# A gated recurrence and a mixer on one core: the last batch's transposes by DMA, and a batch's inputs loaded ahead of the second weight

## The chip, the core and the metric

The kernel runs on one core of a Trainium2 chip. A core has five engines that run their own instruction queues side by side: TensorE (PE, matrix products into PSUM), VectorE (DVE), ScalarE (ACT), GpSimd (POOL) and SyncE (SP, which here only starts transfers). Sixteen DMA engines carry the transfers. The on-chip memory is SBUF with 128 partitions, and PSUM with 8 banks, where PE writes its results. A semaphore makes one engine wait for another. The metric is the time of one execution in microseconds (us); less is better.

## The reference

Four batches (B), eight heads (H), 768 time steps (S), head dimension 48 (D). The first part is a recurrence with a gate alpha, the second a mixer: a low-rank mix over time, then a two-layer network over the 384 channels.

```python
    for t in range(S):
        state = alpha[:, :, t, :, None] * state + np.einsum('bhd,bhe->bhde', k[:, :, t], v[:, :, t])
        y[:, :, t] = np.einsum('bhd,bhde->bhe', q[:, :, t], state)
...
    x = np.ascontiguousarray(attn_out.transpose(0, 2, 1, 3)).reshape(B, S, H * D)
...
    xt = x.transpose(0, 2, 1)
    h = xt @ U @ V
    u = x + h.transpose(0, 2, 1)
    ch = np.maximum(u @ w_ch1, 0.0) @ w_ch2
    return (u + ch).astype(np.float32)
```

x is 4 x 768 x 384, U and V have rank 32 and act over time, the two layers go from 384 to 1536 channels and back. All inputs and the output are float32.

## The kernel before

**Tiling.** Time is cut in six chunks of 128 steps, taken two at a time, so a batch has three groups. Within a chunk the recurrence is written with matrix products. The logarithm of alpha is summed over time by a product with a triangle of ones (L358; L360 gives the chunk's total). Exponentials of plus and minus that sum (`aa`, `ai`) scale q and k (`rq`, `rk`, L374). Both are transposed so that the head dimension lies on the partitions (`qT`, `kT`): PE transposes eight 128x128 blocks into a PSUM bank (L383), and ACT or DVE copies the bank to SBUF (L289, L291). Then come the scores (L406), a mask on DVE (`pm`, L416), the state (L441, L448, L451) and y (L468, L474), which ACT copies into `xb` (L486). `rv` is v cast to bf16 on POOL (L291).

After a batch's three groups comes the mix, `stage_mix`: a product with U over all six chunks (L499), its copy `utx`, then for each chunk a product with V (L524) that DVE adds to `xb` (L525). That gives u. PE transposes u in three blocks of six (L534), ACT copies them to `uT` (L542). The two layers are `mlp1` (L553, 72 matmuls a batch of 384 columns, in two halves of time of 36, with a ReLU on ACT or DVE, L563 and L565) and `mlp2` (L574, again 72), whose result DVE adds to u in one of three `ou` buffers (L583) and SP stores (L584). The first batch does u's transposes in another way (L515, L518).

**Loads.** Each batch has four loads of 1.2 MB in the order alpha, k, q, v, each into one of six `io` buffers (L327). Between the first and the second batch's come U, V (four copies) and the weights in three parts each, w1 and w2, through two parts to an `io` buffer; POOL casts them to bf16.

**What sets the order.** Each step is an operation handed to a planner with its engine, a cost in ns and a priority (`P.add`). The planner simulates all engines with these costs, always takes the step that can start first (and the lowest priority number among those), gives it its buffers, and so writes each engine's fixed order. On the chip each engine follows its own order and waits by semaphores. SP in particular takes its transfers strictly in turn: one that waits for its data holds all behind it. For SP the planner keeps a clock of the sequencer and one of the transfers:

```python
            if eng == "SP":
                clock[eng] = max(t + 450.0, dma)
                dma = max(dma, t + 1200.0) + op.cost
                op.end = dma + 1700.0
```

Loads have the batch's number as priority (alpha of batch b: b, k: b + 0.1, and so on), the parts of w1 0.5, of w2 0.6, the stores -1. Attention steps have 1000 to 1110, the mix 500 to 530, the layers 5000 and up, so PE fills with the layers of one batch the time in which the next batch's recurrence waits.

Of the kernel before, what the change touches and what calls it, by code (L numbers as in the profile page):

```python
# [49 lines left out]
class Op:  # L50
    __slots__ = ("eng", "cost", "fn", "prio", "deps", "bufs", "n", "end", "users", "est", "i")


class Plan:
# [11 lines left out]
    def add(self, eng, cost, fn, r=(), w=(), prio=0.0, after=(), kind=None):  # L66
        op = Op()
        op.eng, op.cost, op.fn, op.prio = eng, cost, fn, prio
        op.i = len(self.ops)
# [31 lines left out]
    def run(self):  # L101
# [13 lines left out]
        while todo:  # L115
# [73 lines left out]
def kernel(  # L189
# [12 lines left out]
    nc = tc.nc  # L202
# [37 lines left out]
    u_in = const.tile([128, NC, R], FP32, name="u_in")  # L240
    vm_in = const.tile([128, S], FP32, name="vm_in")
# [16 lines left out]
    pms = Pool(slots("pm", 4, [C, 2, HP, C], BF16))  # L258
# [3 lines left out]
    uts = Pool(slots("uT", 2, [128, NCT, S], BF16))  # L262
# [17 lines left out]
    mlps = [every, every, every, every]  # L280
# [12 lines left out]
    def load_low_rank():  # L293
        P.add("SP", 500, lambda: nc.sync.dma_start(u_in, moe_U.rearrange("(c p) r -> p c r", p=128)), w=["u_in"], prio=0.3)
        for g in range(4):
            P.add("SP", 400, lambda g=g: nc.sync.dma_start(vm_in[32 * g : 32 * g + R, :], moe_V), w=[("vm_in", g)], prio=0.3)
        P.add("POOL", 350, lambda: nc.gpsimd.tensor_copy(u_sb, u_in), r=["u_in"], w=["u"], prio=300)
        P.add("POOL", 820, lambda: nc.gpsimd.tensor_copy(vm_sb, vm_in), r=[("vm_in", g) for g in range(4)], w=["vm"], prio=300)

    def load_big():  # L300
# [6 lines left out]
        for i, (src, dst) in enumerate(parts):  # L307
# [7 lines left out]
            P.add("SP", 2000, lambda src=src, stage=stage: nc.sync.dma_start(stage(), src), w=[(t, i)], prio=0.5 if i < 3 else 0.6)  # L315
# [14 lines left out]
    def stage_gla(b, g, sprev, xb, ins):  # L330
# [8 lines left out]
        eq = "DVE" if first else "POOL"  # L339
        ev = "POOL"  # L340
        eqt = "ACT" if first else "DVE"
        split = (-1, 1, 1)[g] if first else -1
# [47 lines left out]
        for src, dst, eng, cost in ((rk, kT, "ACT", 1015), (rq, qT, eqt, 1015 if eqt == "ACT" else 640)):  # L390
            tb = Buf(gen)
# [100 lines left out]
    def stage_mix(b, xb, uT):  # L492
# [14 lines left out]
        if b == 0:  # L507
            P.fill_end = op
            for hf in range(2):
                for j in range(NCT):  # L510
# [9 lines left out]
                    P.add(eng, 550 if eng == "DVE" else 490, lambda hf=hf, j=j, tb=tb, eng=eng: copy(eng, uT()[:, j, hf * TW : (hf + 1) * TW], tb()[:, 0, 0:TW]), r=[tb], w=[(uT, hf, j)], prio=pr)  # L520
# [112 lines left out]
```

## Time and profile before

| | us |
|---|---|
| median of 3 runs | 181.5 (180.69 to 182.88) |
| the profiled execution | 180.38 |
| its span, first to last instruction | 178.7 |
| PE busy in the span | 166.2 |
| POOL, DVE, ACT busy | 52.7, 94.0, 86.5 |

The profiled execution lies a little under the fastest of the three runs. Its span is 1.7 us shorter than its time. The mean granted clock of TensorE is 0.989 of full speed.

How to read it: the page cuts the span into 40 slices of 4.5 us and gives each engine's busy share in tenths. A window row gives the same for a stretch that is named in us. A row of the time order gives start and length of an instruction, the idle time of its engine before it and, after the arrow, what ended that idle time. The chain follows, from the last instruction back, what each waited for. Of the loads, the first rows that use a tile tell when it had landed.

### The profile page before, as it was taken

Reading aid. Unit: us, or ns where it says so; the run is one execution under the profiler, and the core shown is the slowest. Engines: PE = TensorE matmul, PEld = TensorE weight load, DVE = VectorE, ACT = ScalarE, POOL = GpSimd, SP = SyncE. Lnnn points to the kernel's source line nnn. Section 1 sums busy time; section 2 is a strip of 40 time slices with the busy share of each in tenths; the row PEclk is TensorE's granted clock in tenths of the full one; section 3 lists DMA queues with packets and bytes.
Section 4 is the critical chain, followed back from the end, with each engine's and each line's share of the span. In section 5 each row is a group of like instructions: output and inputs, shape, how many; then the busy total and the mean of one; then the engine's idle time right before and its main releaser. Section 6 shows DMA issues by size and latency. Waiting matters only on the chain.

```text
span 178.7 us, 4275 instructions
## 1 busy us (share of the span) xinstructions
PE 166.2 (93%) x1821; PEld 107.8 (60%) x1821; DVE 94.0 (53%) x159; ACT 86.5 (48%) x142; POOL 52.7 (29%) x52
## 2 busy tenths in 40 slices
PE   5997888999999996988999999999999999999992
PEld 4775665555666754655666566755566565656560
DVE  2022991643327775458676577667485432544421
ACT  2387684645891344894783847401555310422200
POOL 4000197760469600497416567000000000000000
PEclk9999999999999999699999999999999999999999
DMA  4987999996977868899889300111101112101212
GB/s 111 262 257 221 261 287 391 370 321 191 261 224 225 254 204 246 275 259 262 257 230 252 117 15 33 48 46 44 48 0 44 48 46 88 44 0 48 85 49 88
DMA packets 32068, 29.08 MB, mean 163 GB/s; under 512 B 1584, under 2 KB 30768, under 8 KB 32048
## 3 DMA queue, kind: packets, MB, share of 16 engines
q1 hardware_dynamic: 32048, 28.81, 53.5%
q8 instruction: 14, 0.23, 0.6%
q14 instruction: 6, 0.05, 0.1%
HBM read 24.08 MB, written 4.72 MB: 161 GB/s over the span
## 4 chain that ended last, share of the span: by engine, by line
PE 65%; DMA 17%; SPq 6%; DVE 5%; ACT 3%; issue 2%; POOL 1%; DVEq 0%; ACTq 0%; POOLq 0%
PE ps L553 24%; PE ps L574 22%; DMA io<-in_alpha_dram 7%; DMA io<-in_q_dram 6%; SPq L327 4%; DMA io<-in_v_dram 4%; PE ps L474 3%; PE ps L383 3%; DVE pm L416 3%; PE ps L406 3%; SPq L584 2%; PE ps L468 2%; PE ps L441 1%; PE ps L524 1%; ACT lt L350 1%
## 5 line engine op out<-in xcount | busy, mean ns | idle before, releaser
L553 PE MATMUL ps<-uT,w_sb 128*128 128x384 bf16 x288 | 52.9, 326 | 0.0
L574 PE MATMUL ps<-w_sb,h1t 128*128 128x384 bf16 x288 | 52.4, 326 | 0.0
L563 ACT ACTIVATE h1t<-ps 128x384 bf16<-128x384 f32 x48 | 23.7, 493 | 37.7 <-PE ps L553 37.4
L574 PEld LDWEIGHTS <-h1t 128*128 128x128 bf16 x288 | 27.2, 98 | 17.1 <-issue 0.3
L553 PEld LDWEIGHTS <-w_sb 128*128 128x128 bf16 x288 | 26.9, 98 | 16.2 <-issue 0.3
L565 DVE TENSOR_SCALAR h1t<-ps 128x384 bf16<-128x384 f32 x48 | 26.7, 557 | 16.6 <-PE ps L553 14.8
L416 DVE TENSOR_TENSOR pm<-ps,maskc 128x1024 bf16<-128x1024 f32 x22 | 26.8, 1221 | 5.5 <-PE ps L406 4.9
L583 DVE TENSOR_TENSOR ou<-xb,ps 128x384 f32<-128x384 bf16 x24 | 13.3, 553 | 29.2 <-PE ps L574 20.5
L374 POOL TENSOR_TENSOR rk<-io,ai 128x768 bf16<-128x768 f32 x9 | 14.8, 1643 | 25.7 <-ACT ai L368 18.9
L289 ACT COPY kt<-ps 128x1024 bf16<-128x1024 bf16 x12 | 12.1, 1015 | 13.1 <-PE ps L383 6.1
L291 POOL CAST rv<-io 128x768 bf16<-128x768 f32 x12 | 9.6, 829 | 23.6 <-DMA io<-in_v_dram 23.6
L486 ACT CAST xb<-ps 128x768 bf16<-128x768 f32 x12 | 9.6, 798 | 13.8 <-PE ps L474 13.7
L374 POOL TENSOR_TENSOR rq<-io,aa 128x768 bf16<-128x768 f32 x9 | 14.8, 1645 | 4.1 <-DMA io<-in_q_dram 2.1
L587 PE MATMUL ps<-fill_in,ident 128*128 128x256 bf16 x87 | 13.6, 316 | 1.9 <-POOL ident masks.py:199 1.9
L350 ACT ACTIVATE lt<-io 128x768 bf16<-128x768 f32 x12 | 9.6, 841 | 9.7 <-DMA io<-in_alpha_dram 9.7
L525 DVE TENSOR_TENSOR xb<-xb,ps 128x384 bf16<-128x384 bf16 x18 | 9.5, 550 | 6.0 <-PE ps L524 5.9
L587 PEld LDWEIGHTS <-ident 128*128 128x128 bf16 x87 | 9.4, 113 | 4.1 <-POOL ident masks.py:199 1.9
L368 ACT ACTIVATE ai<-ps 128x768 bf16<-128x768 f32 x12 | 9.9, 822 | 0.3 <-PE ps L360 0.3
L369 ACT ACTIVATE aa<-ps 128x768 bf16<-128x768 f32 x12 | 10.0, 830 | 0.0
L291 POOL CAST w_sb<-io 128x1536 bf16<-128x1536 f32 x6 | 8.8, 1469 | 3.9 <-DMA io<-in_moe_w_ch_dram 3.9
L474 PE MATMUL ps<-rv,pm 128*128 128x48 bf16 x192 | 8.9, 184 | 1.1 <-DVE pm L416 1.1
L406 PE MATMUL ps<-qt,kt 48*128 48x128 bf16 x192 | 9.0, 218 | 0.5 <-ACT xb L486 0.5
(57 smaller groups left out, 157.4 us busy)
## 6 DMA issues: line engine op xcount, KB each, us to landing
io<-in_moe_w_ch_dram SPq DMA_DIRECT2D x6, 768.0 KB, 9.7
out_dram<-ou SPq DMA_DIRECT2D x24, 192.0 KB, 1.9
vm_in<-in_moe_V_dram SPq DMA_DIRECT2D x4, 96.0 KB, 2.6
u_in<-in_moe_U_dram SPq DMA_DIRECT2D x1, 96.0 KB, 6.1
io<-in_alpha_dram SPq DMA_DIRECT2D x4, 0.2 KB, 11.3
io<-in_k_dram SPq DMA_DIRECT2D x4, 0.2 KB, 10.2
io<-in_q_dram SPq DMA_DIRECT2D x4, 0.2 KB, 10.5
io<-in_v_dram SPq DMA_DIRECT2D x4, 0.2 KB, 8.9
```

The source lines that it names most:

```text
L289: nc.scalar.copy(dst, src)
L291: ENG[eng].tensor_copy(dst, src)
L374: ENG[eng].tensor_tensor(dst()[:, :, :, 0:D], ch(src), fac().rearrange("t g (h d) -> t g h d", d=D), op=ALU.mult)
L406: nc.tensor.matmul(s2[:, par, p, :], lhsT=kT()[o : o + D, i, p, :], rhs=qT()[o : o + D, i, p, :], start=(p == 0), stop=(p == HP - 1),)
L416: nc.vector.tensor_tensor(pmi().rearrange("t two hp c -> t (two hp) c"), sc().rearrange("p two (hp c) -> p (two hp) c", c=C), maskc.to_bro ...
L474: nc.tensor.matmul(y2[:, par, p, :], lhsT=pm[i]()[:, par, p, :], rhs=rv()[:, i, 2 * p + par, :], start=(i == 0 and p == 0 and last is None ...
L553: nc.tensor.matmul(hb()[:, 0, 0:TW], lhsT=w1_sb[:, ct, jt * 128 : (jt + 1) * 128], rhs=uT()[:, ct, tt * TW : (tt + 1) * TW], start=(ct == ...
L563: P.add("ACT", 500, lambda jt=jt, hb=hb: nc.scalar.activation(h1()[:, jt, :], hb()[:, 0, 0:TW], AF.Relu), r=[hb], w=[(h1, jt)], prio=100)
L565: P.add("DVE", 560, lambda jt=jt, hb=hb: nc.vector.tensor_scalar_max(h1()[:, jt, :], hb()[:, 0, 0:TW], 0.0), r=[hb], w=[(h1, jt)], prio=100)
L574: nc.tensor.matmul(hb()[:, 0, 0:DM], lhsT=h1()[:, jt, (c % 3) * C : (c % 3 + 1) * C], rhs=w2_sb[:, jt, :], start=(jt == 0), stop=(jt == NJ ...
L583: P.add("DVE", 550, lambda: nc.vector.tensor_tensor(ou(), xb()[:, c, :], hb()[:, 0, 0:DM], op=ALU.add), r=[hb, (xb, c)], w=[ou], prio=100)
L587: P.fill_fn = lambda i: nc.tensor.matmul(ps[:, i, 0:256], lhsT=ident, rhs=fill_in, start=True, stop=True)
```

## The change

Four things are changed in what runs, and the planner's order follows from them.

1. In the last batch (b = 3), k's and q's transposes of all three groups are done by SP as DMA transposes from `rk` and `rq` into `kT` and `qT`, in place of PE's eight blocks and a copy each. u's transposes in that batch are two DMA transposes of three chunks each, in place of three PE blocks and copies. `uT` is laid out chunk by chunk for that.
2. In the second batch (b = 1), q is scaled on DVE and no longer on POOL, and q's transposed blocks are copied by ACT and no longer by DVE.
3. The parts of w2 get priority 1.15 in place of 0.6, so that alpha and k of the second batch (1.0 and 1.1) go ahead of them.
4. U and V go through an `io` buffer and not tiles of their own; there are six `pm` buffers in place of four. The matmul that adds the mix at the end of `mlp2` in the first batch is a step of its own. Priorities of the first batch's `mlp1` are closer together, so all of it can stand ahead of `mlp2`.

The planner is told for a DMA transpose how long it holds SP (`hold`).

```diff
-                clock[eng] = max(t + 450.0, dma)
+                clock[eng] = max(t + op.hold, dma)
...
-    pms = Pool(slots("pm", 4, [C, 2, HP, C], BF16))
+    pms = Pool(slots("pm", 6, [C, 2, HP, C], BF16))
...
-    uts = Pool(slots("uT", 2, [128, NCT, S], BF16))
+    uts = Pool(slots("uT", 2, [128, NC, NCT, C], BF16))
...
-        P.add("SP", 500, lambda: nc.sync.dma_start(u_in, moe_U.rearrange("(c p) r -> p c r", p=128)), w=["u_in"], prio=0.3)
+        P.add("SP", 500, lambda: nc.sync.dma_start(u_in(), moe_U.rearrange("(c p) r -> p c r", p=128)), w=[(t, 4)], prio=0.3)
...
-            P.add("SP", 2000, lambda src=src, stage=stage: nc.sync.dma_start(stage(), src), w=[(t, i)], prio=0.5 if i < 3 else 0.6)
+            P.add("SP", 2000, lambda src=src, stage=stage: nc.sync.dma_start(stage(), src), w=[(t, i)], prio=0.5 if i < 3 else 1.15)
...
-        eq = "DVE" if first else "POOL"
+        eq = "DVE" if b in (0, 1) else "POOL"
         ev = "POOL"
-        eqt = "ACT" if first else "DVE"
+        eqt = "ACT" if b in (0, 1) else "DVE"
...
         for src, dst, eng, cost in ((rk, kT, "ACT", 1015), (rq, qT, eqt, 1015 if eqt == "ACT" else 640)):
+            if b in (3,):
+                P.add("SP", 1000, lambda src=src, dst=dst: nc.sync.dma_start_transpose(dst().rearrange("p g e c -> p (g e) c"), src().rearrange("t g h w -> t (g h w)")), r=[src], w=[dst], prio=pr / 1000 - 1, hold=1250.0)
+                continue
...
+            if b in (3,):
+                if c % 3 == 2:
+                    P.add("SP", 1100, lambda c=c: nc.sync.dma_start_transpose(uT()[:, c - 2 : c + 1].rearrange("p c j t -> p (c j) t"), xb()[:, c - 2 : c + 1, :].rearrange("p c m -> p (c m)")), r=[(xb, c - i) for i in range(3)], w=[(uT, c // 3, j) for j in range(NCT)], prio=pr / 1000 - 1, hold=1300.0)
+                continue
...
-            pr = 5000 + b * 1000 + tt * 100 + jt * 8
+            pr = 5000 + b * 1000 + tt * (100 if b else 50) + jt * (8 if b else 4)
...
-                        rhs=uT()[:, ct, tt * TW : (tt + 1) * TW], start=(ct == 0), stop=(ct == NCT - 1),
+                        rhs=uT()[:, 3 * tt : 3 * tt + 3, ct, :], start=(ct == 0), stop=(ct == NCT - 1),
```

How the order moves: first SP's queue from V's copies on, at the end of the first batch's loads. A row is the line, the transfer with the tile written and the one read, and their shape; `w_ch` are the weights, 3x512 a part of w1, 4x384 of w2; `io` buffers are told apart by their number. Before:

```order
L296 DMA vm_in<-in_moe_V_dram 32x768 x4
L315 DMA io_90<-in_moe_w_ch_dram 128x3x512 x2
L315 DMA io_91<-in_moe_w_ch_dram 128x3x512
L315 DMA io_91<-in_moe_w_ch_dram 128x4x384
L315 DMA io_86<-in_moe_w_ch_dram 128x4x384 x2
L327 DMA io_87<-in_alpha_dram 128x48x48
L327 DMA io_88<-in_k_dram 128x48x48
L327 DMA io_89<-in_q_dram 128x48x48
L584 DMA out_dram<-ou_149 128x384
L584 DMA out_dram<-ou_150 128x384
L327 DMA io_90<-in_v_dram 128x48x48
L327 DMA io_91<-in_alpha_dram 128x48x48
```

The same place in the changed kernel:

```order
L321 DMA io_89<-in_moe_w_ch_dram 128x3x512 x2
L321 DMA io_84<-in_moe_w_ch_dram 128x3x512
L333 DMA io_85<-in_alpha_dram 128x48x48
L333 DMA io_86<-in_k_dram 128x48x48
L321 DMA io_84<-in_moe_w_ch_dram 128x4x384
L321 DMA io_87<-in_moe_w_ch_dram 128x4x384 x2
L333 DMA io_88<-in_q_dram 128x48x48
L333 DMA io_89<-in_v_dram 128x48x48
L333 DMA io_84<-in_alpha_dram 128x48x48
L596 DMA out_dram<-ou_149 128x384
```

Alpha and k have moved ahead of w2's three parts, and v and the third batch's alpha ahead of the stores, of which three now follow together.

Second, POOL's queue from the cast of w1 on, through the second batch. Before:

```order
L291 CAST w_sb<-io_91 128x3x512
L291 CAST w_sb<-io_91 128x1536
L291 CAST w_sb<-io_86 128x1536 x2
L374 TENSOR_TENSOR rk_101<-io_88,ai_118 128x16x48
L374 TENSOR_TENSOR rk_98<-io_88,ai_119 128x16x48
L374 TENSOR_TENSOR rq_95<-io_89,aa_115 128x16x48
L374 TENSOR_TENSOR rq_96<-io_89,aa_116 128x16x48
L374 TENSOR_TENSOR rk_99<-io_88,ai_120 128x16x48
L374 TENSOR_TENSOR rq_97<-io_89,aa_117 128x16x48
L291 CAST rv_112<-io_90 128x768
```

In the changed kernel:

```order
L289 CAST w_sb<-io_84 128x3x512
L380 TENSOR_TENSOR rk_99<-io_86,ai_116 128x16x48
L289 CAST w_sb<-io_84 128x1536
L380 TENSOR_TENSOR rk_96<-io_86,ai_117 128x16x48
L289 CAST w_sb<-io_87 128x1536 x2
L380 TENSOR_TENSOR rk_97<-io_86,ai_118 128x16x48
L289 CAST rv_110<-io_89 128x768
```

The casts of w2 (128x1536) now stand between the three k products of the second batch, and the three q products have left POOL. In the third batch POOL now does the third k product ahead of its first cast of v, and in the last one all casts of v ahead of the third group's k and q.

Third, SP's queue from the last batch's v on, where there were only stores before:

```order
L333 DMA io_85<-in_v_dram 128x48x48
L398 DMA_TRANSPOSE kt_123<-rk_97 128x8x128
L596 DMA out_dram<-ou_149 128x384
L398 DMA_TRANSPOSE qt_126<-rq_93 128x8x128
L398 DMA_TRANSPOSE kt_124<-rk_98 128x8x128
L596 DMA out_dram<-ou_150 128x384
L398 DMA_TRANSPOSE qt_127<-rq_94 128x8x128
L398 DMA_TRANSPOSE kt_125<-rk_99 128x8x128
L398 DMA_TRANSPOSE qt_128<-rq_95 128x8x128
L596 DMA out_dram<-ou_151 128x384
```

The six transposes of k and q stand behind the last load, with stores of the second batch between them. u's two follow later among the third batch's stores.

On PE, the 66 transposes of the last batch are gone (48 for k and q, 18 for u), and the rest is dealt out anew. All 72 matmuls of the first batch's `mlp1` now stand ahead of the first of its `mlp2`. Between the mixes (L499) of the second and the third batch PE's queue held 51 matmuls of `mlp1` and 12 of `mlp2`; now it holds 60 and 24, one block of sums (L358) more and two blocks of eight transposes less. The last batch's first scores stand after the third batch's mix, three matmuls of `mlp1` and eight of `mlp2` between them.

More of the change, by code (lines that the diff above doesn't have):

```diff
@@ L50 @@
 class Op:
-    __slots__ = ("eng", "cost", "fn", "prio", "deps", "bufs", "n", "end", "users", "est", "i")
+    __slots__ = ("eng", "cost", "fn", "prio", "deps", "bufs", "n", "end", "users", "est", "i", "hold")
 class Plan:
@@ L279 @@
     mlp0 = banks((6,), (7,), (4,), (5,))
-    mlps = [every, every, every, every]
+    mlps = [banks(*[(i,) for i in s]) for s in (range(8),) * 4]
     def bf(bank):
@@ L569, in mlp2 @@
         pr = 5000 + b * 1000 + 100 + (c % 3) * 33 + (0 if c < 3 else 100)
-        for g in range(3):
+        for g in range(NJ // 4):
             def f(g=g):
-                for jt in range(4 * g, 4 * g + 4):
+                for jt in range(4 * g, 4 * (g + 1)):
                     nc.tensor.matmul(
@@ L577, in f @@
                     )
-                if g == 2 and utx is not None:
-                    nc.tensor.matmul(hb()[:, 0, 0:DM], lhsT=vm_sb[:, c * C : (c + 1) * C], rhs=utx(), start=False, stop=True)
-            P.add("PE", mm(*[DM] * (5 if g == 2 and utx is not None else 4)), f, r=([utx] if utx is not None else []) + [(h1, jt) for jt in range(4 * g, 4 * g + 4)] + [("w2", g)], w=[hb], prio=pr + g)
+            P.add("PE", mm(*[DM] * 4), f, r=[(h1, jt) for jt in range(4 * g, 4 * (g + 1))] + [("w2", g * 4 // 4)], w=[hb], prio=pr + g)
+        if utx is not None:
+            P.add("PE", mm(DM), lambda: nc.tensor.matmul(hb()[:, 0, 0:DM], lhsT=vm_sb[:, c * C : (c + 1) * C], rhs=utx(), start=False, stop=True), r=[utx], w=[hb], prio=pr + 9)
         ou = Buf(outs)
```

34 lines of the change are left out of this document (18 added, 16 removed).

## The prediction

> **What bounds the kernel now.** I read the page's busy shares and slices first, then the chain that ended last, then the windows in which PE (TensorE) is not full, and last the time order of the engines in those windows. The page:
>
> ```profile
> PE 166.2 (93%) x1821; PEld 107.8 (60%) x1821; DVE 94.0 (53%) x159; ACT 86.5 (48%) x142; POOL 52.7 (29%) x52
> PE   5997888999999996988999999999999999999992
> PEclk9999999999999999699999999999999999999999
> PE 65%; DMA 17%; SPq 6%; DVE 5%; ACT 3%; issue 2%; POOL 1%; DVEq 0%; ACTq 0%; POOLq 0%
> ```
>
> PE is busy for 93% of the 178.7 us; no other engine is above 60%. The chain is PE for 65% and transfers and their queue (DMA, SPq) for 23%. Where each rules is in the windows (columns: length; busy us and count of PE, weight loads, DVE, ACT, POOL; granted clock, DMA share, GB/s):
>
> ```profile
> 65.00:70.00 5.00, 3.71 (x85) 2.60 (x84) 3.85 (x6) 2.99 (x4) 0.00 (x0) 1.00 0.86 246
> 72.00:77.00 5.00, 4.46 (x39) 3.03 (x36) 2.86 (x6) 4.11 (x8) 3.06 (x2) 0.66 0.80 236
> 80.00:85.00 5.00, 3.97 (x64) 2.54 (x57) 4.26 (x6) 2.35 (x5) 3.87 (x5) 1.00 0.91 257
> 85.00:90.00 5.00, 5.00 (x86) 3.09 (x83) 3.44 (x7) 4.01 (x7) 1.97 (x2) 1.00 0.85 243
> 110.00:120.00 10.00, 10.00 (x114) 6.45 (x112) 5.72 (x11) 2.96 (x6) 0.98 (x1) 1.00 0.09 32
> ```
>
> From 85 us on PE has no idle time: matmuls taken out there shorten the kernel by their own length. Between 65 and 85 us PE idles 1.29 us in the first row, 0.54 in the second and 1.03 in the third, and in the second its clock is 0.66, which costs another 0.34 x 5 = 1.7 us. Up to the load of the third part of w1, at about 28 us, the order of no queue changes. What PE waits for between 65 and 85 us stands in the time order of POOL (start, length, instruction, idle time before it and its releaser):
>
> ```profile
> 34.40 1.47 POOL L291 CAST w_sb<-io 128x1536 bf16<-128x1536 f32 x1 [0.66 <-DMA io<-in_moe_w_ch_dram]
> 46.98 3.42 POOL L374 TENSOR_TENSOR rk<-io,ai 128x768 bf16<-128x768 f32 x2 [6.71 <-PE ps L553]
> 51.97 3.25 POOL L374 TENSOR_TENSOR rq<-io,aa 128x768 bf16<-128x768 f32 x2 [1.56 <-DMA io<-in_q_dram]
> 59.03 2.37 POOL L291 CAST rv<-io 128x768 bf16<-128x768 f32 x3 [0.62 <-DMA io<-in_v_dram]
> 81.41 1.60 POOL L291 CAST rv<-io 128x768 bf16<-128x768 f32 x2 [1.13 <-DMA io<-in_v_dram]
> 95.55 1.64 POOL L374 TENSOR_TENSOR rq<-io,aa 128x768 bf16<-128x768 f32 x1 [0.58 <-DMA io<-in_q_dram]
> 100.08 2.37 POOL L291 CAST rv<-io 128x768 bf16<-128x768 f32 x3 [2.89 <-DMA io<-in_v_dram]
> ```
>
> POOL waits for loads: v of the second batch lands at 59.03 us, of the third at 81.41, q and v of the last at 95.55 and 100.08. So the loads set the pace up to 85 us, and PE after it.
>
> **Term 1: transposes off PE, -3.7 us.** The last batch loses six blocks of 8 transposes (k and q of three groups) and three blocks of 6 (u), 66 matmuls. In the chain (start, length, what) they cost, among neighbours that PE runs without a gap:
>
> ```profile
> 97.87 0.45 PE ps L383 x8
> 111.64 0.34 PE ps L534 x6
> 128.24 0.43 PE ps L499 x6
> 169.27 5.86 PE ps L574 x36
> ```
>
> 6 x 0.45 + 3 x 0.34 = 3.7 us. In the program before, the last batch's stand in the full stretch: the chain's last piece on PE, from 169.27, ends without a wait. All 3.7 us are on the path, unless a transfer that replaces them comes late (below).
>
> **What is hidden, 0.** The copies out of PSUM go too, three each of these, the kt ones on ACT, the qt ones on DVE, the uT ones on ACT:
>
> ```profile
> L289 ACT COPY kt<-ps 128x1024 bf16<-128x1024 bf16 x12 | 12.1, 1015 | 13.1 <-PE ps L383 6.1
> 54.56 0.69 DVE L291 COPY qt<-ps 128x1024 bf16<-128x1024 bf16 x1 [0.54 <-PE ps L383]
> 133.05 0.80 ACT L542 COPY uT<-ps 128x768 bf16<-128x768 bf16 x1 [0.49 <-PE ps L534]
> 19.16 0.95 DVE L374 TENSOR_TENSOR rk<-io,ai 128x768 bf16<-128x768 f32 x1
> ```
>
> That is 3 x (1.015 + 0.69 + 0.80) = 7.5 us of engines that PE does not wait for after 85 us: nothing gained. The other layout of uT, PSUM copies with the same element count, the two input tiles in an io slot, the last matmul of a group as a step of its own, and two more pm buffers cost nothing that a row prices; PE hides none of it because none of it adds work to PE.
>
> **Term 2: the loads, -0.6 - 0.9 + 0.4 us.** The second batch's alpha and k go ahead of the three parts of w2, its v and the third batch's alpha ahead of three stores that now follow them. A load takes 46.98 to 51.97, 5.0 us (the first row's wait is put down to a matmul long done; it is k that lands), or 95.55 to 100.08, 4.5 us. So alpha and k come earlier by w2's three parts, some 6 us, q as before, and v, no longer behind two stores, about one load after q: 56.5 to 57 in place of 59.03. POOL is rid of three multiplications of 1.64 us (q of that batch goes to DVE, 0.95 us each by the last row above; its qT copies go from DVE to ACT, which is busy for half of that time). The attention of the second batch can thus run 2 to 3 us earlier, but PE has the same matmuls to do up to there, so no more than its 1.29 us of idle time at 65 to 70 us can go. Where it sits the chain shows:
>
> ```profile
> 65.03 2.31 ACT lt L350 x3
> 67.33 0.69 ACT xb L486
> 68.07 0.41 PE ps L406 x8
> 68.58 1.24 DVE pm L416
> ```
>
> PE's scores at 68.07 wait for ACT's copy into xb, which stands behind the three logarithms of the third batch's alpha (landed at 65.03); with that alpha some 4 us earlier this wait, 0.5 us, goes. The mask after the scores, 1.24 us on DVE before PE can go on, stays for the most part: -0.6 in all. Bounds 0 and -1.3.
>
> In 80 to 85 us PE idles 1.03 us, behind v of the third batch (81.41) and the POOL work queued behind it. By the order, that load has one interruption by stores less ahead of it, and POOL does the third k before v: -0.9. Bounds: 0, and all 1.03. The stretch between, where PE waits for one batch's mix step by step at clock 0.66, keeps its order: 0. Bounds: the lost 1.7 us could go or occur a second time.
>
> The price: w2's casts, the first at 34.40 now, come two loads later, 43.4 to 44.4 us, and stand on POOL between rk steps of 1.64 us. When does PE need them?
>
> ```profile
> 32.59 6.40 PE ps L553 x39
> 38.99 1.30 PE ps L574 x8
> 45.88 0.16 PE ps L358
> 46.12 0.18 PE ps L358
> ```
>
> A matmul of the first layer takes 6.40 / 39 = 0.164 us, one of the second 1.30 / 8 = 0.163, a sum block (two L358, with small ones behind each) 0.5. PE now does all 72 of the first layer ahead of w2, 11.8 us, and two sum blocks and one transpose block, 1.5 us, so it needs w2 at 32.4 + 13.3 = 45.7 us. The first part is cast at 43.4 + 1.47 = 44.9 to 45.9 us; the second k follows on POOL, 1.64 us, and PE's second transpose block waits for it: 46.5 to 47.5 us, where PE would be at 46.4. Wait 0 to 1.6 us in all; I take 0.4, since the casts of parts two and three find PE with first-part work of three chunks in hand.
>
> **Term 3: do the DMA transposes land in time? 0 us.** No row shows a DMA transpose. One moves 128 rows of 1,024 bf16, 256 KB. The nearest rows (size, median us to landing; then SP's issues):
>
> ```profile
> out_dram<-ou SPq DMA_DIRECT2D x24, 192.0 KB, 1.9
> io<-in_v_dram SPq DMA_DIRECT2D x4, 0.2 KB, 8.9
> 85.04 4.36 SPq L327 DMA_DIRECT2D io<-in_q_dram  x1
> 89.86 4.18 SPq L327 DMA_DIRECT2D io<-in_v_dram  x1
> ```
>
> A store of 192 KB lands in 1.9 us. A load is 128 x 48 = 6,144 runs of 192 bytes and holds SP about 4.2 us, 0.7 ns a run. If a transpose went by runs of 128 elements, its 1,024 runs would take 0.7 us; if by single elements, 131,072 of them, 90 us. Those are the ends. By size and place (on chip, long rows) it is nearest to the store; I take 2 to 3 us each, one after another. They also queue behind v of the last batch, issued until 94.04 and landed at 100.08, so the first lands no sooner than about 102, and q's, whose product is ready at 95.55 + 1.64 = 97.2, by 106 at 3 us each.
>
> When does PE need them? It starts the third batch's mix at 100.82:
>
> ```profile
> 100.82 0.43 PE ps L499 x6
> ```
>
> By the order, the stretch of PE's queue between the second and third mix now holds 9 more first-layer and 12 more second-layer matmuls (21 x 0.163 = 3.4 us), one more sum block (0.5 us) and two transpose blocks less (0.9 us): +3.0. With the gains of term 2 the third mix starts at 100.82 - 1.1 + 3.0 = 102.7, and 3.4 us of matmuls later (the mix's own 0.4, three first-layer and 8 second-layer ones, 1.8, and small ones) come the last batch's first scores: 106.1. At 3 us each both transposes are there; the limit is (106.1 - 100.1) / 2 = 3.0 us. The sixth is needed 16.4 us of matmuls later (40 of the second layer and 30 of the first, 11.4 us, and some 5 us of small ones, by the order), at 122.5, the limit (122.5 - 100.1) / 6 = 3.7 us. u's two transposes have 14 us of matmuls between the last sum and the first use. SP also holds stores behind transposes: a late store blocks an ou buffer, DVE's next ou, and then PE's bank; the three ou buffers cover some 6 us of second-layer work. Cost 0; the ends are 0 and tens of us.
>
> On this the Trainium skill speaks against the change. "VectorE: DVE Perf Modes", section "The three transpose paths", gives 1,309 ns for one 128x128 block by DMA; eight blocks in a row are, as an estimate from that page, 10.5 us for one of these transposes, and the sum would be +36 us instead of -4.8. "Advanced Engine Details and Errata", section "X-Bar Transpose (TRN2)", says that such transfers go as fast as ordinary ones, by which the sum stands. No run here shows either.
>
> **Sum.** -3.7 - 0.6 - 0.9 + 0.4 = -4.8 us. The profiled execution took 180.38 us (span 178.7): 175.6. It lies 1.1 us under the median of the runs (181.5) and 0.3 under the fastest (180.69); from these the sum gives 176.7 and 175.9. I predict 176.2.
>
> **Rivals.**
> - *Slow transposes* (slower). A DMA transpose moves its blocks one after another; with T us each PE stalls on the last batch's scores, 6 T - 22.4 us by the sixth. It eats the gain at T = 4.5 and makes the kernel slower by over 1% at T = 4.9. At 6 us: 176.2 + 13.6 = 190. For it: the finest pieces in the trace (192-byte runs) are what holds SP longest. Against it: the store's 1.9 us. By the page with 1,309 ns, 10.5 us each, it would be 217. Chance 0.16.
> - *Only the matmuls* (smaller gain). The loads gain nothing, since the waits at 65 to 85 us are a chain of mask, copy and mix; the w2 wait is at its upper end: -3.7 + 0 to 1.6: 178 to 179.4. For it: clock 0.66 and DVE at 3.85 of 5 us at 65 to 70. Chance 0.14.
> - *New waits eat it* (within 1%). PE's wait for w2 at 46 to 50 us, 1.6 us, brings a second stretch at clock 0.66 (1.7 us), or T is 4.2 to 4.8: -3.7 + 3.3 = -0.4: about 181. Against it: PE has work of 0.65 us blocks between those waits. Chance 0.11.
>
> The forecast holds the other 0.59, with its own range 173.5 to 178 (the bounds: the clock's 1.7 us won, to half of term 2 lost).
>
> **Chances.** About 1% (1.8 us) is what a measurement of this kernel tells from no change. Faster by more: the forecast, and the second rival where it stays under 179.7: 0.73. Within: 0.11. Slower: 0.16. The range reaches from 173.4 to 181.0; what is left out is the slow rival and a little at the fast end.
>
> **What would show it.** Right: PE's 66 transposes gone and its busy time about 3.7 us less; transposes that land in under 3 us; no PE wait before the last batch's scores; v of the second batch cast near 57 us; PE full from about 83 us to the end. Wrong: a PE wait on a DMA into kt or qt; SP held by a transpose over 4 us; w2's casts after 47 us with PE idle; the clock low in a second stretch.

## The result, and the profile after

| | before | changed |
|---|---|---|
| median | 181.91 us (180.69 to 182.88, 4 runs) | 176.22 us (174.97 to 176.74, 4 runs) |
| ratio, with its 95% interval | | 0.968 (0.960 to 0.976) |
| profiled execution | 180.38 us, span 178.7 | 174.97 us, span 173.3 |
| PE busy, matmuls | 166.2 us, 1821 | 160.6 us, 1755 |

The changed kernel is 5.7 us faster by the medians, 5.4 us between the two profiled executions. Here and below a median is over all executions, while a ratio and its interval leave out slow ones, those more than 1.5% above the fastest of their kernel. The page of the changed kernel (busy shares, slices):

```profile
PE 160.6 (93%) x1755; PEld 102.1 (59%) x1755; DVE 92.4 (53%) x156; ACT 84.5 (49%) x139; POOL 47.7 (28%) x49
PE   5988797999879989889999999999999999999991
PEclk9999999999999999999999999999999999999999
```

PE is still the engine at 93%, and from the 19th slice on (78 us) it is full. The 66 matmuls are gone. PE's busy time fell by 5.6 us, more than their 3.7: the clock row has no 6 any more, which was worth up to 1.7 us. The windows that the prediction read, now in the changed kernel (length; busy us and count of PE, weight loads, DVE, ACT, POOL; granted clock, DMA share, GB/s):

```profile
65.00:70.00 5.00, 5.00 (x76) 2.93 (x73) 4.20 (x6) 0.80 (x1) 0.00 (x0) 1.00 0.89 252
72.00:77.00 5.00, 4.09 (x52) 2.91 (x51) 3.09 (x6) 5.00 (x10) 4.67 (x3) 1.00 0.73 226
80.00:85.00 5.00, 4.99 (x63) 2.91 (x60) 4.72 (x8) 2.11 (x5) 4.38 (x5) 1.00 0.81 235
```

The idle time of PE at 65 to 70 us (1.29 us before) and at 80 to 85 us (1.03) is gone, and the clock at 72 to 77 is 1.00 where it was 0.66. What came instead stands at 46 to 65 us in PE's time order (start, length, instruction, idle time before it and its releaser); the first row is the start of the first batch's first layer, the last two are the mix and the first first-layer matmul of the second batch:

```profile
32.04 5.59 PE L564 MATMUL ps<-uT,w_sb 128*128 128x384 bf16 x33
...
46.57 0.62 PE L389 MATMUL ps<-ident,rk 128*128 128x128 bf16 x8 [0.45 <-POOL rk L380]
...
50.55 0.81 PE L586 MATMUL ps<-w_sb,h1t 128*128 128x384 bf16 x4 [0.88 <-POOL w_sb L289]
...
64.77 0.24 PE L457 MATMUL ps<-st,ident 128*128 128x192 bf16 x1 [0.53 <-DVE st L460]
...
71.10 0.79 PE L508 MATMUL ps<-xb,u_sb 128*32 128x384 bf16 x6
...
77.58 0.65 PE L564 MATMUL ps<-uT,w_sb 128*128 128x384 bf16 x3
```

The same three places in the kernel before:

```profile
32.43 6.56 PE L553 MATMUL ps<-uT,w_sb 128*128 128x384 bf16 x39
...
70.67 0.79 PE L499 MATMUL ps<-xb,u_sb 128*32 128x384 bf16 x6
...
78.23 0.65 PE L553 MATMUL ps<-uT,w_sb 128*128 128x384 bf16 x3
```

PE waits 0.45 us for the k product that stands between w2's casts and 0.88 us for w2's third part, 1.33 us together, and 0.53 us for a state on VectorE (`st`). The second mix comes 0.43 us later than before in spite of the earlier loads, although the first layer began 0.39 us earlier, so from the first layer to the second mix the changed kernel takes 0.82 us longer. From there to the second batch's first layer it then takes 6.48 us, not 7.56. POOL in the changed kernel shows when loads are there:

```profile
43.45 1.46 POOL L289 CAST w_sb<-io 128x1536 bf16<-128x1536 f32 x1 [1.26 <-DMA io<-in_moe_w_ch_dram]
...
49.02 1.47 POOL L289 CAST w_sb<-io 128x1536 bf16<-128x1536 f32 x1 [1.10 <-DMA io<-in_moe_w_ch_dram]
...
57.31 2.37 POOL L289 CAST rv<-io 128x768 bf16<-128x768 f32 x3 [5.22 <-DMA io<-in_v_dram]
```

SP's queue around the transposes (start, time that the issue holds SP), and the times from issue to landing (count, median us):

```profile
89.36 4.10 SPq L333 DMA_DIRECT2D io<-in_v_dram  x1
93.58 5.24 SPq L398 DMA_TRANSPOSE kt<-rk  x1
98.92 1.06 SPq L596 DMA_DIRECT2D out_dram<-ou  x1
100.08 1.30 SPq L398 DMA_TRANSPOSE qt<-rq  x1
101.52 1.24 SPq L398 DMA_TRANSPOSE kt<-rk  x1
```

```profile
kt<-rk SPq DMA_TRANSPOSE x3, 4.4
qt<-rq SPq DMA_TRANSPOSE x3, 4.2
uT<-xb SPq DMA_TRANSPOSE x2, 3.2
```

Behind a store or another transpose, a transpose of 256 KB mostly holds SP 1.24 to 1.43 us (once 2.34); it lands 3.2 to 7.9 us after its issue (the median is 4.3 over the six, and 3.2 for u's two), and the next is issued meanwhile. PE has no wait on one. The third mix and the last batch's first scores, in the chain (start, length, what):

```profile
102.03 0.43 PE ps L508 x6
...
105.39 0.33 PE ps L415 x8
```

The third mix starts 102.03 - 100.82 = 1.2 us later than before, with the 3.0 us of work more ahead of it that the prediction counted, so 1.8 us were gained by then. Of these +0.43 stand at the second mix and -1.1 between it and the second batch's first layer; the rest, -1.1, came after that, up to 85 us, where PE's idle time of 1.03 us is gone. With -3.7 for the matmuls the sum is -5.5, against -5.4 measured.

### The profile page after: what moved, and what is told of

Its sections match the earlier page's. It is cut to its first block, busy times and chain, and to the rows that moved or that the text cites. A ratio compares the mean times of both kernels' runs of the same rounds, so it can differ in the third digit from the quotient of the medians.

```text
span 173.3 us, 4151 instructions
## 1 busy us (share of the span) xinstructions
PE 160.6 (93%) x1755; PEld 102.1 (59%) x1755; DVE 92.4 (53%) x156; ACT 84.5 (49%) x139; POOL 47.7 (28%) x49
## 2 busy tenths in 40 slices
DMA packets 40771, 31.23 MB, mean 180 GB/s; under 512 B 10288, under 2 KB 39472, under 8 KB 40752
## 4 chain that ended last, share of the span: by engine, by line
PE 58%; SPq 19%; DMA 12%; ACT 4%; DVE 3%; issue 1%; ACTq 0%
PE ps L586 22%; PE ps L564 21%; SPq L333 15%; DMA io<-in_q_dram 6%; DMA io<-in_alpha_dram 6%; SPq L321 3%; PE ps L415 3%; PE ps L483 3%; PE ps L389 2%; DVE pm L425 2%; PE ps L477 2%; PE ps L533 1%; PE ps L450 1%; ACT lt L356 1%; ACT ai L374 1%
## 5 line engine op out<-in xcount | busy, mean ns | idle before, releaser
L586 PE MATMUL ps<-w_sb,h1t 128*128 128x384 bf16 x288 | 53.2, 326 | 0.9 <-POOL w_sb L289 0.9
L599 PE MATMUL ps<-fill_in,ident 128*128 128x256 bf16 x87 | 12.6, 298 | 1.9 <-POOL ident masks.py:199 1.9
L599 PEld LDWEIGHTS <-ident 128*128 128x128 bf16 x87 | 8.8, 107 | 3.5 <-POOL ident masks.py:199 1.9
L380 POOL TENSOR_TENSOR rq<-io,aa 128x768 bf16<-128x768 f32 x6 | 9.9, 1643 | 2.6 <-DMA io<-in_q_dram 2.6
L287 ACT COPY kt<-ps 128x1024 bf16<-128x1024 bf16 x9 | 9.1, 1024 | 1.9 <-PE ps L389 1.9
L460 DVE TENSOR_TENSOR st<-ps,tot 128x192 bf16<-128x192 f32 x20 | 7.0, 352 | 4.6 <-PE ps L457 4.0
## 6 DMA issues: line engine op xcount, KB each, us to landing
io<-in_k_dram SPq DMA_DIRECT2D x4, 0.2 KB, 10.5
```

Of the source, the lines that this page charges most:

```text
L380: ENG[eng].tensor_tensor(dst()[:, :, :, 0:D], ch(src), fac().rearrange("t g (h d) -> t g h d", d=D), op=ALU.mult)
L586: nc.tensor.matmul(hb()[:, 0, 0:DM], lhsT=h1()[:, jt, (c % 3) * C : (c % 3 + 1) * C], rhs=w2_sb[:, jt, :], start=(jt == 0), stop=(jt == NJ ...
L599: P.fill_fn = lambda i: nc.tensor.matmul(ps[:, i, 0:256], lhsT=ident, rhs=fill_in, start=True, stop=True)
```

## The experiments

Edits are against the changed kernel unless said otherwise; in these kernels the line numbers are 3 or 7 higher than in the changed one. Where a kernel names the batches in a variable, the diff shows them written out. The planner deals the order out anew for each edit, so an edit to the loads or to an engine moves more than its own line.

### The parts alone

Only the transposes by DMA; the loads' order, the second batch's q and the first layer's priorities as before:

```diff
-            P.add("SP", 2000, lambda src=src, stage=stage: nc.sync.dma_start(stage(), src), w=[(t, i)], prio=0.5 if i < 3 else 1.15)
+            P.add("SP", 2000, lambda src=src, stage=stage: nc.sync.dma_start(stage(), src), w=[(t, i)], prio=0.5 if i < 3 else 0.6)
...
-        eq = "DVE" if b in (0, 1) else "POOL"
-        eqt = "ACT" if b in (0, 1) else "DVE"
+        eq = "DVE" if first else "POOL"
+        eqt = "ACT" if first else "DVE"
...
-            pr = 5000 + b * 1000 + tt * (100 if b else 50) + jt * (8 if b else 4)
+            pr = 5000 + b * 1000 + tt * 100 + jt * 8
```

> Only the DMA transposes of the last batch (k, q, u) are kept; the loads' order, the engines of the second batch's q and the first batch's mlp1 priorities are as before. Theory A (the 66 transposes were on the path of a full PE and nothing else of them counts): 3.7 us less than before, ratio 0.980. Theory B (the gain needs the earlier loads as well, since without them the transposes land late or PE waits elsewhere): less than 2 us, ratio over 0.989. Profile: PE busy time 3.7 us less, no PE wait on a transfer into kt, qt or uT.

Measured: 178.09 us, ratio 0.979 (0.972 to 0.986), as theory A has it. The profile bears out that PE waits for no transfer into kt, qt or uT. Its other sign, 3.7 us less of PE's busy time, can't be read there: that execution took 183.3 us and had the half clock twice (mean 0.962). And the other half, all transposes on PE, the loads and q as changed:

```diff
-            if b in (3,):
+            if b in ():
```

> The reverse: all transposes back on PE, the loads' order and the second batch's q on DVE as in the changed kernel. Theory A, by the prediction's terms: 0.6 + 0.9 - 0.4 = 1.1 us less than before, ratio 0.994. By the trace of the changed kernel (second batch's mix 0.4 us later, later waits 1.2 us less, and 1.1 us less where the clock was low before): 0.8 us less if the low clock comes and goes from run to run, 1.9 us if the order removed it, ratio 0.996 or 0.990. Rival: the wait for w2 eats it, ratio 1.0 or more.

Measured: 179.97 us, ratio 0.992 (0.989 to 0.996), between the two values of theory A, and a gain, unlike the rival. The halves add up within the intervals: 0.979 x 0.992 = 0.971, the whole 0.968. About two thirds of the gain or a little more are the transposes, the rest the loads, q and the first layer's priorities. The small edits of point 4 of the change (buffers, the step of its own) are in both halves and were not run alone.

Then two parts of the second half, the transposes left on DMA and the first layer's new priorities kept in both. First w2 ahead of the second batch's alpha and k again (the first piece of the first diff):

> The changed kernel with the second part of the weights loaded ahead of the second batch's alpha and k, as before; q of that batch stays on VectorE and the transposes on DMA. Theory order (the 1.4 us of the loads' half come from the order of the loads): 177.5 to 178.2, ratio 0.976 to 0.98, with PE idle again at 65 to 70 and at 80 to 85 us. Rival, q on VectorE (POOL, rid of three multiplications of 1.64 us, is what lets v be cast early): 176 to 176.7, ratio 0.968 to 0.971.

Measured: 179.93 us, ratio 0.990 (0.984 to 0.996), slower than either theory had it. And q of the second batch on POOL again (its second piece):

> The changed kernel with q of the second batch scaled on POOL and its transposes' copies on VectorE, as before; the loads' new order and the DMA transposes stay. Theory order: POOL has the room, 176 to 176.8, ratio 0.968 to 0.972. Rival, q on VectorE is what gives the 1.4 us: 177.3 to 178.2, ratio 0.975 to 0.98, with v of the second batch cast after 59 us and PE idle at 65 to 70 us.

Measured: 179.76 us, ratio 0.985 (0.977 to 0.993). Neither theory holds. With the transposes made by DMA, the new order without q on VectorE, or q on VectorE without the new order, is no better than neither (178.09, ratio 0.979); both together give 176.0 to 176.2. One difference is left in this comparison: the kernel with neither also has the first layer's old priorities. With the new ones all 72 matmuls of the first batch's first layer stand ahead of the second layer even where w2 is loaded early (the first second-layer matmul is at 48.43 us with the old place of w2, at 38.83 in the kernel before), so the kernel with the old place of w2 may pay for the new priorities without using the early w2. What the priorities are worth by themselves was not run. The windows of the kernel with the old place of w2, and PE's waits in that with q on POOL:

```profile
65.00:70.00 5.00, 4.47 (x91) 2.79 (x88) 3.80 (x5) 2.63 (x4) 0.00 (x0) 1.00 0.82 237
70.00:75.00 5.00, 3.96 (x75) 2.88 (x72) 3.39 (x5) 1.08 (x2) 0.00 (x0) 0.59 0.83 248
75.00:80.00 5.00, 4.96 (x57) 2.90 (x54) 2.22 (x5) 4.85 (x9) 3.51 (x3) 0.73 0.82 232
80.00:85.00 5.00, 3.86 (x58) 2.76 (x57) 2.62 (x6) 4.04 (x7) 4.00 (x4) 1.00 0.89 250
```

```profile
51.43 0.81 PE L589 MATMUL ps<-w_sb,h1t 128*128 128x384 bf16 x4 [1.16 <-POOL w_sb L292]
65.16 0.81 PE L589 MATMUL ps<-w_sb,h1t 128*128 128x384 bf16 x4 [0.78 <-DVE ou L598]
71.84 0.37 PE L486 MATMUL ps<-rv,pm 128*128 128x48 bf16 x8 [0.86 <-DVE pm L428]
...
89.86 0.65 PE L567 MATMUL ps<-uT,w_sb 128*128 128x384 bf16 x3 [1.08 <-ACT h1t L578]
106.19 0.40 PE L418 MATMUL ps<-qt,kt 48*128 48x128 bf16 x8 [0.51 <-DMA qt<-rq]
```

With the old place of w2 the pattern of the kernel before is back: idle at 65 to 70 and at 80 to 85, and the low clock between (mean 0.66 over 10 us, a loss of up to 3.4 us). With q on POOL the order of loads is the new one and the clock stays at 1.00, but PE waits in five places that the changed kernel does not have at that size, two of them on VectorE (ou, pm) before 72 us. So early loads seem to pay only if POOL and VectorE are dealt out to match; the waits point to it, no run shows it by itself. Why the old place of w2 alone stays at 179.9 and not at 178.1 is not settled: the low clock and the new priorities can each account for it, that is one profile, and the intervals touch.

### How much slower could a transpose be?

The prediction had the k and q transposes harmless up to 3.0 or 3.7 us each. So each was made twice, first into a spare tile, with four `pm` buffers (as before the change) to make room; the other engines' order is the same.

```diff
+    def dma_tr(dst, src):
+        for x in spare:
+            nc.sync.dma_start_transpose(x.rearrange("p g e c -> p (g e) c"), src)
+        nc.sync.dma_start_transpose(dst, src)
```

> The changed kernel with each of the six DMA transposes of k and q made twice, the first into a spare tile (two pm buffers fewer make room; the order of all other engines is the same). If a transpose holds SP 1.25 us and lands about 2 us after that, a pair takes 2.5 us and q's first one lands near 105.7 us, where PE wants it at 105.4: 0 to 0.5 us slower than the changed kernel. If its price were its 3.2 to 4.4 us to landing, one after another, 6 x 6.4 = 38 us would pass until the sixth and PE would wait over 15 us.

Measured: 181.88 us, ratio 1.004 (0.999 to 1.008): 5.7 us lost, the whole gain, where the prediction's limits say no loss; it lies between the two values expected here. PE's waits beyond 85 us in this kernel, its windows, and SP's queue at the end of the transposes:

```profile
106.89 0.40 PE L422 MATMUL ps<-qt,kt 48*128 48x128 bf16 x8 [1.49 <-DMA qt<-rq]
122.68 1.01 PE L571 MATMUL ps<-uT,w_sb 128*128 128x384 bf16 x3 [2.71 <-DVE ou L602]
```

```profile
120.00:125.00 5.00, 2.32 (x14) 0.88 (x13) 2.92 (x5) 0.49 (x1) 0.00 (x0) 0.78 0.65 199
125.00:130.00 5.00, 5.00 (x72) 2.91 (x72) 3.51 (x6) 1.78 (x3) 0.00 (x0) 0.88 0.00 0
```

```profile
118.34 1.33 SPq L246 DMA_TRANSPOSE qt<-rq  x1
119.76 3.23 SPq L603 DMA_DIRECT2D out_dram<-ou  x4
```

PE waits 1.49 us for the first q, and 2.71 us on VectorE's `ou`. That second wait begins on SP: four stores stand behind the sixth transpose until 119.76 us, the first of which goes out at 109.29 in the changed kernel. Its `ou` buffer is not free, VectorE's next `ou` cannot be written, and PE's bank is not emptied. With the low clock after it, (0.22 + 0.12) x 5 = 1.7 us, the sum is 5.9, beside 5.7 measured. Three transposes each:

> The same with three of each, 3.75 us a group. The prediction's rule (first scores when two groups are done, 100.1 + 2 T against 106.1; the sixth at 100.1 + 6 T against 122.5) gives a wait of 1.5 us: 1.5 us slower than the changed kernel. With the stores that stand between the transposes on SP (about 1 us each) and 2 us of landing added, q's first lands near 108.3 (PE at 105.4) and the sixth near 124.5 (PE at 119): 5 to 6 us slower, in PE waits on transfers into qt.

Measured: 187.34 us, ratio 1.035 (1.026 to 1.043), 11.1 us lost, twice what the larger of the two estimates had; these are two executions. The same two waits grow to 4.45 and 3.76 us, and the clock is 0.67 in the 5 us after the first and 0.70 around the second. Where SP issues little but transposes, the window of this kernel shows how fast they move:

```profile
115.00:120.00 5.00, 5.00 (x41) 3.30 (x39) 2.52 (x6) 1.60 (x2) 0.00 (x0) 1.00 1.03 201
```

If the stores are the cause of the second wait, a fourth `ou` buffer takes it away and leaves the first, with the transposes still made twice:

```diff
-    outs = Pool(slots("ou", 3, [C, DM], FP32))
+    outs = Pool(slots("ou", 4, [C, DM], FP32))
```

> Each of the six k and q transposes of the last batch is still made twice, but there is a fourth ou buffer. Theory stores (the three ou buffers are what cannot stand slower transposes: a store behind six transposes on SP keeps an ou buffer, VectorE's next ou waits, PE's bank waits, 2.7 us plus the low clock after it): the wait of PE on ou is gone, the wait of 1.5 us on the first q transpose stays, so the time is 176.2 + 1.5, with a little low clock 177.5 to 179, ratio 0.976 to 0.985. Rival, the transposes themselves load the DMA engines or hold the chain of scores (the ou wait is only where the delay shows): the time stays at 181 to 182.5, ratio about 1.0, with PE waiting as long at other instructions.

Measured: 179.04 us, ratio 0.985 (0.978 to 0.993). Its only PE wait after 100 us:

```profile
108.90 0.40 PE L422 MATMUL ps<-qt,kt 48*128 48x128 bf16 x8 [2.56 <-DMA qt<-rq]
```

The wait on `ou` is gone and the clock stays at 1.00 there; the loss over the changed kernel, 2.8 us, is about the wait for q, here 2.56. All engines but SP run the same sequence of instructions in both kernels. So half of the loss of the doubled transposes was the `ou` buffers, as the theory of the stores had it. The wait for q was larger than expected, so the time lies at the upper edge of the forecast.

### The changed kernel again, and more transposes by DMA

Four kernels on one chip: the changed one unaltered; u of the third batch by DMA too; k, q and u of the third batch; u of the second and third. The edit is which batches stand in the conditions, for u alone:

```diff
-            if b in (3,):
+            if b in (2, 3):
                 if c % 3 == 2:
```

> The changed kernel once more, unaltered. Theory order: the wait of 0.88 us for the second part of the weights near 50 us and the later second mix are the price of the new order of loads and show again at their size. Rival, loads land differently from one execution to the next: that wait is gone or differs by half a microsecond while the order is the same, and the time stays at 175 to 177, ratio 0.966 to 0.972.

Measured: 175.96 us, ratio 0.970 (0.964 to 0.975). The order is the same to the instruction, but PE's wait for w2 is not there, and the clock is low at another place:

```profile
20.00:25.00 5.00, 4.96 (x71) 3.67 (x71) 4.00 (x4) 3.31 (x4) 2.40 (x4) 0.66 0.90 219
...
30.00:35.00 5.00, 4.80 (x63) 3.19 (x58) 0.57 (x2) 2.09 (x5) 3.82 (x3) 0.66 1.05 328
...
45.00:50.00 5.00, 5.00 (x44) 3.36 (x42) 2.23 (x4) 4.51 (x10) 4.80 (x4) 1.00 1.08 350
```

PE is busy 163.3 us here, 2.7 more than in the first profile, yet the time is 0.9 longer. While PE is behind, w2 lands in time: the low clock takes the place of the wait. In all eleven profiles with the new order it is so: in the five with a low clock at some place between 20 and 40 us PE does not wait for w2, in the six with the full clock it waits 0.72 to 1.16 us. So neither theory: the wait is the price of the order, and it shows at full clock; a low clock ahead of it hides it and, by these two profiles, costs little more than it.

u of the third batch by DMA as well, on two occasions:

> The third batch's u is transposed by DMA too (three blocks of 6 transposes and their copies fewer; two more transposes on SP, one of them among the last batch's q and k). Theory A (PE is full there, each matmul taken out shortens the kernel by its length, and a transpose of 1.25 us on SP still fits): 3 x 0.34 = 1.0 us less, 175.2, ratio 0.963 to 0.966. Theory stores (the SP queue is near its limit around 105 to 115 us, where twice the transposes cost 5.7 us): one more transpose ahead of the store of the third ou buffer brings 0 to 1.3 us of wait: 175.2 to 176.5, with a PE wait on ou or on the first-layer matmuls of the third batch in the trace.

Measured: 174.36 us, ratio 0.960 (0.953 to 0.968).

> The kernel with the third batch's u by DMA too, again, beside the changed kernel on the same chip. Theory A: 1.0 us (3 x 0.34) under the changed kernel of this call, that is a ratio smaller by 0.005 to 0.006. Rival: no difference that can be told from zero.

Measured: 174.42 us, ratio 0.963 (0.957 to 0.969), 1.5 us under the changed kernel on the same chip. The intervals against before still overlap, but over both occasions 11 executions have a mean of 174.7 (standard deviation 0.8), and the 10 of the changed kernel 176.0 (0.7). It has the lowest median here; the expected 1.0 us is within what was seen, and no PE wait after 82 us shows in either profile.

> k, q and u of the third batch go by DMA as well as those of the last (66 more matmuls off PE, 3.7 us by the same rows). Theory A (only PE's matmuls count): 172.5, ratio 0.948 to 0.953. Theory queue (SP is in order: six transposes, each waiting for its product on POOL, now stand ahead of the last batch's alpha, k, q and v loads, at least 6 x 1.25 = 7.5 us, and the last batch's first scores had about 1 us to spare): PE waits for the last batch some 3 to 7 us, and the time is 176 to 181, ratio 0.967 to 0.995, with SP held by a transpose for over 2 us before a load and DMA share down near 70 to 95 us.

Measured: 174.99 us, ratio 0.965 (0.959 to 0.971): by the medians 1.0 us under the changed kernel, of the 3.7 that the matmuls were worth, and the intervals overlap. The longer of PE's waits beyond 80 us, and SP's queue where the third batch's second transpose stands behind a load:

```profile
85.86 0.62 PE L418 MATMUL ps<-qt,kt 48*128 48x128 bf16 x16 [1.82 <-DMA qt<-rq]
...
113.63 0.31 PE L453 MATMUL ps<-rv,rk 128*64 128x48 bf16 x8 [0.66 <-DVE ou L598]
...
114.88 0.66 PE L567 MATMUL ps<-uT,w_sb 128*128 128x384 bf16 x3 [0.40 <-DMA uT<-xb]
```

```profile
77.23 0.71 SPq L336 DMA_DIRECT2D io<-in_v_dram  x1
78.06 5.66 SPq L401 DMA_TRANSPOSE qt<-rq  x1
```

With two smaller ones (0.23 and 0.19) that is 3.3 us of waits, all on transposes or on `ou`, as much as the gain that is missing. Waits at the low end of those expected came as the queue's theory says; its time, 176 to 181, did not.

> u of the second, third and last batch by DMA; the second batch's two transposes stand on SP ahead of the last batch's k, q and v loads. Theory A (PE's matmuls only): 2.0 us under the changed kernel, 174.2, ratio 0.957 to 0.961. Theory queue: these loads come 2.6 us and a wait for the second batch's u later, PE waits for the last batch's first transposes: 176 to 179, ratio 0.967 to 0.985, worse than with the u of two batches.

Measured: 180.91 us, ratio 0.994 (0.990 to 0.999): 5 us worse than the changed kernel, more than either theory. The row of SP and those of the windows:

```profile
80.40 7.17 SPq L540 DMA_TRANSPOSE uT<-xb  x2
```

```profile
75.00:80.00 5.00, 2.23 (x33) 1.44 (x32) 2.82 (x4) 2.70 (x5) 4.81 (x4) 0.99 0.85 253
80.00:85.00 5.00, 4.14 (x48) 3.71 (x48) 4.30 (x6) 1.37 (x2) 5.00 (x6) 0.50 0.94 263
85.00:90.00 5.00, 4.91 (x74) 3.14 (x73) 3.86 (x6) 2.73 (x6) 0.51 (x1) 0.50 0.83 160
90.00:95.00 5.00, 5.00 (x59) 3.18 (x59) 0.98 (x3) 2.42 (x5) 0.00 (x0) 0.50 0.79 231
```

The damage is not where the queue theory put it, at the last batch. The two transposes stand behind the load of the last batch's alpha and hold SP 7.17 us, and PE begins the second batch's first layer at 88.37 us, where with its own transposes it began at 77.58. At 75 to 80 us PE then has nothing to fill its waits for POOL and VectorE with (2.77 us idle of 5), and 15 us at half clock follow. Of these waits 1.55 us is for q of the third batch, whose load landed later than in the changed kernel; whether by chance, one profile doesn't tell.

## Why the prediction came out right

The time was predicted at 176.2 us, and 176.22 was measured. That closeness is luck: the sum was a gain of 4.8 us, and the gain is 5.4 us between the profiled executions and 5.7 by the medians, with a median of before that came out 0.4 us above the one the prediction had. The direction, the range and the main term are not luck. Term by term:

- **Term 1, -3.7.** Right. From 85 us on PE is full in both kernels, and the 66 matmuls count with their whole length. The transposes alone gave 181.9 - 178.1 = 3.8 us. The copies cost nothing when they went, as said.
- **Term 2, the loads.** Predicted up to the second mix: -0.6 + 0.4 = -0.2; measured +0.43. The loads came as worked out (v cast at 57.31, predicted 56.5 to 57; first cast of w2 at 43.45, predicted 43.4 to 44.4), and the idle time at 65 to 70 us went, all 1.29 us of it where 0.6 was expected. Ahead of the first layer 0.39 us had been won where no order had changed; the profiles at full clock begin it anywhere from 32.0 to 33.2 us, so that looks like chance, and the term itself came out at +0.43 + 0.39 = +0.82. The mis-sized piece is the wait for w2, taken as 0.4: it is 1.33 us at full clock, within the bounds of 0 to 1.6. It was taken low because PE was thought to have second-layer work in hand, with w2's first part, until parts two and three were cast; it had not enough by the third, whose cast ends at 49.02 + 1.47 = 50.49 us: the wait of 0.88 us at 50.55. So the sign "w2's casts after 47 us with PE idle", listed among the wrong ones, did show. The wait of 0.53 us for `st` was in no term. At 80 to 85 us the prediction had -0.9, and -1.1 came.
- **The low clock, 0.** The prediction kept the stretch at 0.66 and put the 1.7 us of it among the bounds. It did not come back: -1.1 us. Over 70 to 80 us the clock is 0.83 before and 0.66 with the old place of w2, and 1.00 in all eleven profiles with the new order. Two against eleven is a strong hint that the order is the cause, no proof.
- **Term 3, 0.** The result is right, its margins are wrong. The signs of transposes landing in under 3 us and of SP held over 4 us by one both came out on the wrong side (medians of 3.2 to 4.4 us, and 5.24 us for the first), and neither cost anything, since transposes overlap and one mostly follows the other after 1.25 us. That is why none is late. But the step that the three `ou` buffers "cover some 6 us", and the limits of 3.0 and 3.7 us, fell: at 2.5 us a transpose the gain is gone. The limits left out the time from issue to landing, 3.2 us or more. And with doubled transposes the stores behind the six go out at 119.76 us and not at 109.29, 10.5 us later, where the `ou` buffers were to cover 6. The reading that a load holds SP 4.2 us, 0.7 ns a run, is doubtful too: see the last section.
- **The sum.** +0.43 - 1.1 - 1.1 - 3.7 stands for the predicted -0.2 + 0 - 0.9 - 3.7. The wait for w2 was under-priced and the clock left out, and these two nearly cancel, which is luck as well.

The rival of slow transposes fell: a transpose costs SP 1.25 us, and PE never waits for one. Yet its turning point was nearer than it said. "Only the matmuls" (178 to 179.4) is the time of the kernel with the transposes alone, 178.09; the loads did add their part. "New waits eat it" had the wait for w2 right in size, but no second stretch at a low clock came with it.

On the transposes the Trainium skill held two rules. "Advanced Engine Details and Errata", section "X-Bar Transpose (TRN2)", says that they are as fast as ordinary transfers. The trace agrees only roughly: with three of each, at 115 to 120 us, the DMA engines are busy throughout (share 1.03) and move 201 GB/s, while the changed kernel's windows with loads have 226 to 252 GB/s at shares of 0.73 to 0.89; and a median landing is 3.2 to 4.4 us against 1.9 for a store. The 1,309 ns for one 128x128 block in "VectorE: DVE Perf Modes", section "The three transpose paths", does not add up over blocks: eight of them take SP 1.25 us here, and even with three of each SP issues one every 1.4 us (nine from 112.86 to 125.20 us).

## What to carry to other kernels

Moving a transpose from a full engine to a DMA pays the matmul's length where nothing late stands behind it, but price it by its place in an in-order queue: its spacing (1.25 us here), its landing (3.2 to 4.4 us), and everything that then issues behind it, down to the store that must free a buffer for another engine. Keep such transposes behind the last loads, and ask at which stage the engine has other work to fill in: u by DMA paid in the third batch and cost 5 us with the second (in the last it was never run apart from k and q). Measure coupled edits together and apart: here taking back either the order of loads or the engine for q lost the whole gain of the two, some 1.4 to 2 us.

## What the runs showed of the hardware

- A transpose issued right behind a load of 192-byte runs holds SP for 5.2 to 6.6 us (5.24 in the changed kernel, 5.66 with k, q and u of two batches, 6.57 with the third batch's u); behind a store or another transpose it is 1.2 to 1.5 us, save one of 1.9 to 2.4 in most kernels. In the kernel with the old place of w2 the first transpose comes 5 us after the last store: 1.36 us. The hold seems to be that of the load ahead and not of the transfer that is issued: in the kernel before, U's load of 96 KB holds SP 4.12 us behind v's load (16.13 us), and a load of 192-byte runs holds it 0.72 us behind stores (51.25). So 4.2 us is not the price of issuing a load by itself.
- The eight transposes raise the packets under 512 bytes from 1,584 to 10,288, about 1,090 for each transpose.
- What makes the granted clock fall is not settled here. A wait of 2.56 us at 108.90 with four `ou` buffers left it at 1.00, one of 2.71 us at 122.68 with three brought 0.78 and 0.88. In the repeated run the low clock at 20 to 25 us begins soon after a wait of 2.15 us (until 19.19), but the one at 30 to 35 us has no idle time of PE longer than 0.49 us in the 3.4 us before it; and with u of three batches the clock stays at 0.50 for 15 us, in the last 5 of which PE is busy without a gap. The Trainium skill, "TensorE: Matmul & The Clock Gate", section "Part 1: The HAM clock gate (the "warmup" mystery)", lets the clock fall after an idle window of some 3.4 us that runs freely. The two waits longer than that, 4.45 and 3.76 us with three of each, both have a low clock at their end or right behind them, as it says; the low clocks after shorter waits it does not cover.
